# The last batch's operand loaded by ScalarE, and fewer conv taps ahead of the copies in stage 2

## The chip, the cores and the metric

The kernel runs on one core of one Trainium2 chip. The metric is the device time in microseconds (us) of one execution. TensorE (PE) multiplies matrices, VectorE (DVE) and ScalarE (ACT) work elementwise and empty the matmul results out of PSUM, GpSimd (POOL) does part of the elementwise work. DMAs are issued by the queue of an engine; in this kernel SyncE (SP) issues nearly all of them.

## The reference

Three layers follow one another on 4 batches. Cut to what matters here:

```python
def reference(...):                        # 4 batches
    a = attn(pooled q, k, v)               # 8 heads, 1152 keys, 576 pooled queries
    x = a as (4, 576, 512)
    # second layer: 4 experts, causal attention over 576 rows, two experts kept per row
    for e in range(4):
        q, k, v = x @ wq[e], x @ wk[e], x @ wv[e]
        ye = softmax(causal(scale * q @ k.T)) @ v @ wo[e]
        out += gate_weight(x, e) * ye
    # third layer: causal convolution of 5 taps as a gate
    gate = sigmoid(sum over k in 0..4 of conv_w[k] * out shifted down by 4 - k rows)
    return (gate * (out @ w_val)) @ w_out
```

## The kernel before

The program has three stages, one for each layer: pooled attention to about 476 us, the expert attention to about 693 us, and the gated product to the end. The change lies in stage 2.

**Stage 2** runs a loop over steps n = 0 to 39 and two more. A step is one batch b (ten steps), one pair of experts g (five steps) and one row tile i; the tiles come in the order 1, 3, 2, 4, 0. In a step the kernel first finishes the softmax weights of step n − 1 on DVE (`norm2`, L844 to L854; POOL then multiplies, L850), has PE make the scores of step n (L814, L821; DVE masks them at L823 and takes the row minimum at L824, L826), and has PE transpose the weights of step n − 2, whose results leave PSUM through `evac`: in turn by ACT (L862) and by DVE (L864, written COPY in the rows). Then come the exponentials of step n on ACT (L835, L837).

**Filler work.** Between these, PE works on a list `fill` of larger pieces, taken one by one by `pop()`: the projections of q and k (`proj`, L242, with the split of the result into a high part on ACT at L224 and a low part on DVE at L225), the values and gate logits (`vgate`, L276), the product with the values (`av2`, L901 and L914), and the product with wo that mixes the experts (`mix`, L936, emptied by ACT at L937 and L938). All of these use four PSUM buffers named a (`ps_m`), as do the transposes. What one piece leaves for other engines goes to the list `late2`, which the next `pop()` empties right behind its own PE work.

**Riders.** After a piece, `ride()` puts one small item on DVE: first what is in `urgent` (the gates, thirteen instructions L294 to L307), otherwise one item of `rides`, at most three in a step (`room = [3]`). The items of `rides` are the taps of the convolution (`tap`, L215), four for each of the four column groups m of a batch, put there when `mix` has finished a group (names x and gp), and a store of gp to memory (L947) in batches 0 and 1. `RD`, by n % 5, says whether the first piece of a step carries a rider at all; this piece stands between the scores and the transposes of the step. Before the change RD is (1, 0, 1, 1, 1).

**Loads and moves.** The operand of a batch, xh, is loaded from memory by `load2`, four DMAs of 576 KB (L196), one for each t. The results of `proj` are copied by `move` to the tiles of the scores: four DMAs for k (L256), six for q (L258, L260, L261 twice), all issued by SP in order. `proj(xh, g, then)` makes k first (w = 1), then q (w = 0). Where it was given `then`, it appends it to `late2` behind the move of q. It is given one only at n = 20, the second pair of batch 1 being over: `then` is `load2(3)`, the load of the last batch.

Of the kernel before, what the change touches and what calls it, by code (L numbers as in the profile page):

```python
# [20 lines left out]
def tile_kernel(ctx, tc, q, k, v, w_gate, wq, wk, wv, wo, w_val, conv_w, w_out, wo_t, q0, k0, out):  # L21
    nc = tc.nc
# [12 lines left out]
    pe, act, dve, pool = nc.tensor, nc.scalar, nc.vector, nc.gpsimd  # L35
# [8 lines left out]
                       fill=1.0, base=0, channel_multiplier=1)  # L44

    x_d = [dram.tile([P, KT, 2, SQ], F32R, name=f"x_d{b}") for b in range(B)]
# [6 lines left out]
                       fill=1e9, base=0, channel_multiplier=1)  # L53
# [10 lines left out]
    def f(ap):  # L64
        return ap.bitcast(F32)
# [124 lines left out]
            late.append(lambda n=n, t=t, c=c, whl=whl: nc.sync.dma_start(f(w3_d[n][:, t, :, c:c + HW]), f(whl)))  # L190
            yield

    def load2(b):
        xh = xh_p.tile([P, KT, 2, SQ], F32R, name="xh")
        for t in range(KT):
            nc.sync.dma_start(f(xh[:, t]), f(x_d[b][:, t]))  # L196
        return [[xh[:, t, i] for i in range(2)] for t in range(KT)]

    def load_part(b, tile_, k):
# [21 lines left out]
    late2, urgent, rides = [], [], []  # L221

    def split2(hi, lo, src, mul=1.0):
        act.activation(hi, src, AF.Copy, scale=mul)  # L224
        late2.append(lambda: dve.scalar_tensor_tensor(out=lo, in0=src, scalar=mul, in1=f(hi), op0=ALU.mult, op1=ALU.subtract))  # L225
# [3 lines left out]
    def proj(xh, g, then=None):  # L229

        box = {}

        def half(w, hf):
            if hf == 0:
                box[w] = hl2.tile([P, 2, SQ], F32R, name="hl")
            hl = box[w]
            cs = slice(w * ED + g * P, w * ED + (g + 1) * P)
            qsl = slice(hf * HQ, (hf + 1) * HQ)
            ps = ps_m.tile([P, 512], F32, name="a")
            ops = [(wi, xi, t) for t in range(KT) for wi, xi in THREE]  # L240
            for o, (wi, xi, t) in enumerate(ops):
                pe.matmul(ps[:, 0:HQ], lhsT=wqk[wi][:, t, cs], rhs=xh[t][xi][:, qsl], start=o == 0, stop=o == len(ops) - 1)  # L242
            split2(hl[:, 0, qsl], hl[:, 1, qsl], ps[:, 0:HQ], -scale if w == 0 else 1.0)
            if hf == 1:
                late2.append(lambda: move(w))
                if w == 0 and then:
                    late2.append(then)

        def move(w):
            hl = box[w]  # L250
            for r in range(2):
                rs = slice(64 * r, 64 * r + 64)
                for i in range(2):
                    src = hl[64 * i:64 * i + 64]
                    if w == 1:
                        nc.sync.dma_start(f(ks[g][i][rs]), f(src))  # L256
                    elif i == 0:
                        nc.sync.dma_start(f(qs[g][0][rs, 0:SQ]), f(src[:, r]))  # L258
                    else:
                        nc.sync.dma_start(f(qs[g][1][rs, 0:4 * P]), f(src[:, r, 0:4 * P]))  # L260
                        nc.sync.dma_start(f(qs[g][1][rs, SQ:]), f(src[:, r, 4 * P:]))  # L261

        return [(1.48, lambda w=w, hf=hf: half(w, hf)) for w in (1, 0) for hf in range(2)]

    def vgate(xh):
# [48 lines left out]
    fill = []  # L314
# [482 lines left out]
    with ExitStack() as s2l:  # L797
# [61 lines left out]
        def evac(dst, src):  # L859
            turn[0] += 1  # L860
            if turn[0] % 2:
                act.activation(dst, src, AF.Copy)  # L862
            else:
                dve.tensor_copy(dst, src)  # L864
# [86 lines left out]

        VG, FD, IN, FL, PEND, PN = 5, 1, 1, 2.6, 7, 3
        GM, VF = (0, 1, 2, 3), (0, 0, 0, 3, 1, 2, 2, 2, 2, 2, 2)
        RD = (1, 0, 1, 1, 1)
        ORDER = (1, 3, 2, 4, 0)
        steps = [(b, g, i) for b in range(B) for g in range(EP) for i in ORDER]
        LAG = 2
# [2 lines left out]
        def ahead(n):  # L960
            return (WORK[steps[n][2]][0] if n < len(steps) else 0) + (WORK[steps[n - LAG][2]][1] if LAG <= n < len(steps) + LAG else 0)
# [34 lines left out]
        for n in range(len(steps) + LAG):  # L996
            if n < len(steps):
                b, g, i = s = steps[n]
                if n % 5 == 0:
                    pts[b, g] = (pt_p2.tile([P, 4, 2, SQ], F32, name="pt"), pt_p2.tile([R64, 2, R64], F32, name="pt4"))  # L1000
                    if g == 0 and b:
                        fill += proj(xh[b], 1, (lambda: xh.update({3: load2(3)})) if b == 2 else None)
                        if b == B - 1:
                            fill.append((0, lambda: late2.append(begin3)))
                    if n == 10 * B - 5:
                        buf = [f(c2.tile([P, 2, SQ], F32R, name=f"k20{i}")) for i in range(2)]
                        bufs = [c2.tile([P, SQ + R64], F32R, name=f"q20{i}") for i in range(2)]
                        v2 = v_p.tile([P, 5, ED + E], F32, name="v2").rearrange("p t c -> p (t c)")
                        first3["raw"] = [[buf[t // 2][:, t % 2] for t in range(KT)], [f(bufs[t])[:, 0:SQ] if t < 2 else v2[:, (t - 2) * SQ:(t - 1) * SQ] for t in range(KT)]]
                        raws = [(0.74, lambda i=i, m=m, hf=hf: value(yhs, i, m, hf, lambda ps, m, qsl: evac(first3["raw"][i][m][:, qsl], ps))) for i in range(2) for m in range(KT) for hf in range(2)]  # L1010
                        fill += raws[0:14]
                    if b == 0 and g == 1:
                        buf = y0_p.tile([P, EP, 2, SQ], F32R, name="y0")
                        yhs.update({(0, i): buf[:, i] for i in range(EP)})
                    if b == 1 and g == 0:
                        buf = y12_p.tile([P, 2, EP, 2, SQ], F32R, name="y12")
                        yhs.update({(1 + j, i): buf[:, j, i] for j in range(2) for i in range(EP)})
                if n % 10 == 5 and b + 1 < B:
                    fill += proj(xh[b + 1], 0)
                if n % 10 == VG and b + 1 < B:  # L1020
                    v2s[b + 1], gws[b + 1], vg = vgate(xh[b + 1])
                    fill += vg
                if n == 0:
                    fill += proj(xh[0], 1)
                if n == FD:
                    fill += [(2.6, lambda g=g: fold(g)) for g in range(EP)]
            t = 0.0
            left = 5 - n % 5
            own = [ahead(m) for m in range(n, n + left)]
            budget = max(FL, (sum(c for c, _ in fill) + (PEND if 10 <= n and n % 10 < PN else 0) + sum(own)) / left) - own[0]  # L1030

            room = [3]

            def ride():
                if urgent:
                    urgent.pop(0)()
                    return
                if rides and room[0]:
                    room[0] -= 1
                    rides.pop(0)()  # L1040

            def pop(rider=True):
                c, a = fill.pop(0)
                now, late2[:] = late2[:], []
                a()
                for x in now:
                    x()
                if rider:
                    ride()
                return c  # L1050

            if 0 <= n - 1 < len(steps):
                norm2(steps[n - 1], gws[steps[n - 1][0]])
            for _ in range({0: 1, 5: 3}.get(n, 0)):
                t += pop()
            if n < len(steps):
                scores2(s)
            if fill:
                t += pop(RD[n % 5])
            else:  # L1060
                flush()
            if n >= LAG:
                b1, g1, i1 = steps[n - LAG]
                transp2(steps[n - LAG], pts[b1, g1])
                if i1 == ORDER[-1]:
                    if g1 == 1:
                        then = (lambda b1=b1: fill.extend(mix(b1, [yhs[b1, 0], yhs[b1, 1]]))) if b1 < B - 1 else begin_last
                    else:
                        then = (lambda: None) if b1 < B - 1 else load_wo3
                    fill[IN:IN] = av2(v2s[b1], pts[b1, g1], g1, yhs[b1, g1], then)  # L1070
            if n < len(steps):
                expo2(s)
            if n == 0:
                flush()
            while fill and t < budget:
                t += pop()
            ride()
            if n == 9:
                xh[2] = load2(2)
            if n in (12, 22):  # L1080
                flush()
            if n % 10 == 9:
                flush()
                while urgent:
                    urgent.pop(0)()
# [123 lines left out]
```

## Time and profile before

| | |
|---|---|
| median of three runs | 761.71 us (761.33 to 763.0) |
| the profiled execution | 761.71 us |
| its span in the trace | 759.9 us |
| granted TensorE clock | 1.0 |
| PE busy, share of the span | 98% |
| DVE busy | 75% |
| ACT busy | 59% |
| POOL busy | 42% |
| chain that ended last | 84% PE, 8% DVE, 3% DMA, 3% ACT |

A row of a timeline gives the start and the length in us, the engine, the line of the kernel, the operation, the tile written, an arrow, the tiles read, the shapes and a count; in brackets stands how long the engine idled just before and what it waited for. Rows of one engine can overlap a little.

### The profile page before, as it was taken

Reading aid. Unit: us, or ns where it says so; the run is one execution under the profiler, and the core shown is the slowest. Engines: PE = TensorE matmul, PEld = TensorE weight load, DVE = VectorE, ACT = ScalarE, POOL = GpSimd, SP = SyncE. Lnnn points to the kernel's source line nnn. Section 1 sums busy time; section 2 is a strip of 40 time slices with the busy share of each in tenths; the row PEclk is TensorE's granted clock in tenths of the full one; section 3 lists DMA queues with packets and bytes.
Section 4 is the critical chain, followed back from the end, with each engine's and each line's share of the span. In section 5 each row is a group of like instructions: output and inputs, shape, how many; then the busy total and the mean of one; then the engine's idle time right before and its main releaser. Section 6 shows DMA issues by size and latency. Waiting matters only on the chain.

```text
span 759.9 us, 14763 instructions
## 1 busy us (share of the span) xinstructions
PE 745.7 (98%) x5317; PEld 616.6 (81%) x5317; DVE 569.4 (75%) x1064; ACT 448.2 (59%) x985; POOL 316.3 (42%) x442
## 2 busy tenths in 40 slices
PE   8999999999999999999999999999999999999998
PEld 7787887787787787877878877988898888878887
DVE  6777888898888988756756766355889797988730
ACT  6665665665665756657656756334564654648632
POOL 6555675675676675652553501022322222220000
PEclk9999999999999999999999999999999999999999
DMA  7876878769778689666657581478425763800212
GB/s 258 254 174 203 226 190 255 211 195 261 209 227 250 187 262 258 178 204 208 166 164 227 132 286 48 111 210 189 135 54 141 199 159 81 267 1 15 84 57 97
DMA packets 83785, 133.52 MB, mean 176 GB/s; under 512 B 19072, under 2 KB 55424, under 8 KB 83712
## 3 DMA queue, kind: packets, MB, share of 16 engines
q1 hardware_dynamic: 83712, 132.58, 61.3%
q8 instruction: 42, 0.69, 0.4%
q14 instruction: 31, 0.25, 0.1%
HBM read 53.37 MB, written 21.76 MB: 99 GB/s over the span
## 4 chain that ended last, share of the span: by engine, by line
PE 84%; DVE 8%; DMA 3%; ACT 3%; issue 1%; SPq 0%; POOL 0%; POOLq 0%; ACTq 0%; DVEq 0%
PE s L440 21%; PE t L489 19%; PE t L519 18%; PE o L1120 7%; PE a L242 5%; PE a L275 4%; PE a L914 2%; DVE gp L215 2%; PE a L779 2%; PE s L814 2%; PE a L886 1%; DMA k<-hl 1%; PE t L478 1%; DVE nm L824 1%; DVE nm L445 1%
## 5 line engine op out<-in xcount | busy, mean ns | idle before, releaser
L452 ACT ACTIVATE p<-s,nm 128x1152 f32<-128x1152 f32 x144 | 176.2, 1223 | 87.9 <-DVE nm L445 85.8
L445 DVE TENSOR_REDUCE nm<-s 128x1 f32<-128x1152 f32 x144 | 192.1, 1352 | 13.9 <-PE s L440 13.6
L489 PE MATMUL t<-ident,p 128*128 128x128 f32 x1296 | 198.8, 275 | 0.7 <-DVE xf L521 0.4
L489 PEld LDWEIGHTS t<-ident,p 128*128 128x128 f32 x1296 | 149.1, 141 | 26.4 <-ACT pt L497 7.0
L497 ACT ACTIVATE pt<-t 128x384 f32<-128x384 f32 x223 | 102.1, 489 | 79.9 <-PE t L489 75.0
L519 PE MATMUL t<-pt,vn 128*64 128x256 f32 (+1 forms) x1152 | 146.7, 408 | 0.0
L499 DVE COPY pt<-t 128x384 f32<-128x384 f32 x209 | 110.9, 554 | 44.5 <-PE t L489 40.5
L519 PEld LDWEIGHTS t<-pt,vn 128*64 128x64 f32 x1152 | 80.0, 137 | 55.9 <-issue 5.2
L440 PE MATMUL s<-ka,qst 128*128 128x384 f32 x384 | 114.6, 380 | 0.2
L440 PE MATMUL s<-kb,qst 128*128 128x384 f32 x384 | 99.1, 367 | 1.7 <-ACT p L452 1.7
L850 POOL TENSOR_TENSOR p<-p,sm 128x512 f32<-128x512 f32 (+3 forms) x32 | 40.2, 1255 | 106.0 <-DVE sm L848 71.3
L440 PEld LDWEIGHTS s<-kb,qst 128*128 128x128 f32 x384 | 60.8, 189 | 15.7 <-issue 13.1
L440 PEld LDWEIGHTS s<-ka,qst 128*128 128x128 f32 x384 | 62.9, 190 | 1.1 <-DVE ka L574 0.9
L377 POOL TENSOR_TENSOR hlk<-kt,hlk 128x384 fp32r<-128x384 f32 x45 | 45.5, 1011 | 1.1
L521 DVE TENSOR_TENSOR xf<-t,rb 128x320 f32<-128x320 f32 (+1 forms) x32 | 14.6, 456 | 41.1 <-PE t L519 40.1
L467 POOL COPY rm<-rs 128x256 f32<-128x256 f32 x31 | 12.4, 401 | 79.3 <-DVE rs L462 77.7
L242 PE MATMUL a<-xh,wqk 128*128 128x288 f32 x288 | 43.3, 300 | 2.1 <-DVE pt L864 2.1
L835 ACT ACTIVATE p<-s,nm 128x256 f32<-128x256 f32 (+3 forms) x64 | 33.1, 524 | 20.3 <-DVE nm L824 20.3
L528 POOL CAST xt<-xf 128x320 fp32r<-128x320 f32 (+1 forms) x32 | 13.6, 426 | 69.9 <-DVE xf L521 69.3
L215 DVE SCALAR_TENSOR_TENSOR gp<-x,cw,gp 128x572 f32<-128x572 f32 (+3 forms) x48 | 40.4, 843 | 2.6 <-ACT gp L938 2.1
L242 PEld LDWEIGHTS a<-xh,wqk 128*128 128x128 f32 x288 | 39.4, 188 | 3.5 <-DVE pt L864 2.5
L440 PE MATMUL s<-hlk,mixed 128*128 128x384 f32 x135 | 33.7, 357 | 0.0
(193 smaller groups left out, 1170.8 us busy)
## 6 DMA issues: line engine op xcount, KB each, us to landing
ka<-hlk SPq DMA_DIRECT2D x90, 192.0 KB, 3.2
kb<-hlk SPq DMA_DIRECT2D x90, 192.0 KB, 3.7
vn<-in_v_dram SPq DMA_DIRECT2D x16, 576.0 KB, 7.2
k<-hl SPq DMA_DIRECT2D x32, 288.0 KB, 4.9
kt<-in_k_dram SPq DMA_DIRECT2D x15, 576.0 KB, 6.1
qt<-in_q_dram SPq DMA_DIRECT2D x15, 576.0 KB, 5.2
qst<-hlq SPq DMA_DIRECT2D x60, 128.0 KB, 3.2
xh<-x_d SPq DMA_DIRECT2D x12, 576.0 KB, 6.0
```

Source lines behind the costliest of these rows:

```text
L215: dve.scalar_tensor_tensor(out=gp[:, n:], in0=x[:, 0:SQ - n], scalar=cw[:, m, c:c + 1], in1=gp[:, n:], op0=ALU.mult, op1=ALU.add)
L242: pe.matmul(ps[:, 0:HQ], lhsT=wqk[wi][:, t, cs], rhs=xh[t][xi][:, qsl], start=o == 0, stop=o == len(ops) - 1)
L377: late.append(lambda: pool.tensor_tensor(out=hlk[:, 1, gs], in0=kt[:, gs], in1=f(hlk[:, 0, gs]), op=ALU.subtract))
L440: pe.matmul(ps[:, 0:GW], lhsT=ops[c][0], rhs=ops[c][1], start=c == 0, stop=c == len(ops) - 1)
L445: dve.tensor_reduce(d["nm"], d["s"][:, :, 0:GW], axis=AX.XY, op=ALU.min)
L452: act.activation(d["p"], d["s"][:, :, 0:GW], AF.Exp, bias=d["nm"], scale=-1.0, accum_out=sums[(2 * n + u) % len(sums)][:, i:i + 1])
L489: pe.transpose(ps[:, j * P:(j + 1) * P], p[:, g, j * P:(j + 1) * P], ident)
L497: act.activation(dst, src, AF.Copy)
L499: dve.tensor_copy(dst, src)
L519: pe.matmul(ps[64 * h:64 * h + 64, 0:N], lhsT=vn[:, h, j, :], rhs=pt[:, j, h, :], start=j == 0, stop=j == C - 1)
L850: pool.tensor_tensor(out=pv, in0=pv, in1=sm[:, :, None].to_broadcast([P, 2, w]), op=ALU.mult)
L1120: pe.matmul(ps[:, 0:w], lhsT=hl[xi][:, kt, t * P - a:(t + 1) * P - a], rhs=end3["wo3"][:, kt, wi, c:c + w], start=o == 0, stop=o == len(op ...
```

## The change

Four edits, all in stage 2:

- `load2` takes the queue to issue from, and the load of the last batch is given ACT's.
- In `proj`, `then` is called at once, when the piece with the second half of q is issued, and no longer put behind the move of q.
- The last entry of `RD` is 0: the first piece of a step with n % 5 = 4 carries no rider.
- `room` is 2 and no longer 3 in the steps with n % 10 of 3 and 4, so that at most two riders go there.

```diff
-    def load2(b):
+    def load2(b, queue=nc.sync):
...
-            nc.sync.dma_start(f(xh[:, t]), f(x_d[b][:, t]))
+            queue.dma_start(f(xh[:, t]), f(x_d[b][:, t]))
...
                 late2.append(lambda: move(w))
                 if w == 0 and then:
-                    late2.append(then)
+                    then()
...
-        RD = (1, 0, 1, 1, 1)
+        RD = (1, 0, 1, 1, 0)
...
-                        fill += proj(xh[b], 1, (lambda: xh.update({3: load2(3)})) if b == 2 else None)
+                        fill += proj(xh[b], 1, (lambda: xh.update({3: load2(3, act)})) if b == 2 else None)
...
-            room = [3]
+            room = [2 if n % 10 in (3, 4) else 3]
```

How the instructions stand on the engines, before and after. The first place is DVE around the end of n = 14, in batch 1 (the numbers behind x are those of the tile). Before:

```order
L215 SCALAR_TENSOR_TENSOR gp<-x_7180,cw,gp 128x572
L215 SCALAR_TENSOR_TENSOR gp<-x_7180,cw,gp 128x573
L215 SCALAR_TENSOR_TENSOR gp<-x_7180,cw,gp 128x574
L844 TENSOR_SCALAR sm<-sm 128x1
L845 RECIPROCAL sm<-sm 128x1
...
L823 TENSOR_TENSOR s<-s,cmask 128x2x128
L824 TENSOR_REDUCE nm<-s 128x2
L215 SCALAR_TENSOR_TENSOR gp<-x_7180,cw,gp 128x575
L864 COPY pt<-a 128x3x128
```

The same place on DVE after the change:

```order
L215 SCALAR_TENSOR_TENSOR gp<-x_7180,cw,gp 128x572
L215 SCALAR_TENSOR_TENSOR gp<-x_7180,cw,gp 128x573
L844 TENSOR_SCALAR sm<-sm 128x1
L845 RECIPROCAL sm<-sm 128x1
...
L823 TENSOR_TENSOR s<-s,cmask 128x2x128
L824 TENSOR_REDUCE nm<-s 128x2
L864 COPY pt<-a 128x3x128
L215 SCALAR_TENSOR_TENSOR gp<-x_7180,cw,gp 128x574
L215 SCALAR_TENSOR_TENSOR gp<-x_7180,cw,gp 128x575
```

Two taps have gone from ahead of the copy of the transposes to behind it. The second place is DVE around the gates (L294 to L307), half a batch later, where the last column group's taps stand (x_7284 before, x_7283 after). The difference, in two pieces:

```order
-L215 SCALAR_TENSOR_TENSOR gp<-x_7284,cw,gp 128x574
 L864 COPY pt<-a 128x3x128
-L215 SCALAR_TENSOR_TENSOR gp<-x_7284,cw,gp 128x575
-L294 TENSOR_TENSOR gt<-v_7308 128x80
...
+L215 SCALAR_TENSOR_TENSOR gp<-x_7283,cw,gp 128x572
+L215 SCALAR_TENSOR_TENSOR gp<-x_7283,cw,gp 128x573
+L294 TENSOR_TENSOR gt<-v_7306 128x80
...
 L824 TENSOR_REDUCE nm<-s 128x2
+L215 SCALAR_TENSOR_TENSOR gp<-x_7283,cw,gp 128x574
 L864 COPY pt<-a 128x8x64
 L225 SCALAR_TENSOR_TENSOR hl<-a,hl 128x288
+L215 SCALAR_TENSOR_TENSOR gp<-x_7283,cw,gp 128x575
```

The last two taps of the batch, which stood ahead of the gates, now stand behind them. The third place is the start of batch 2 (n = 20 and on), on SP, the queue that issues the moves of k and q, and on ACT. SP, the difference:

```order
-L947 DMA g_d_71<-gp 128x576 x2
-L256 DMA k_6178<-hl 64x1152
...
-L258 DMA q_6174<-hl 64x576
-L260 DMA q_6175<-hl 64x512
...
-L196 DMA xh<-x_d_70 128x1152 x4
...
+L256 DMA k_6179<-hl 64x1152
+L947 DMA g_d_71<-gp 128x576
+L258 DMA q_6174<-hl 64x576
```

The four loads are gone from behind the q moves, and one store of gp stands between the k and the q moves. ACT there:

```order
 L835 ACTIVATE p,sm<-s,nm 128x512 x2
 L224 ACTIVATE hl<-a 128x288
+L196 DMA xh<-x_d_70 128x1152 x4
 L902 ACTIVATE y_7003<-a 128x128
 L224 ACTIVATE y_7003<-a 128x448
```

The four loads have come in ahead of the first product with the values (L902). In the changed program the first, third and fifth q moves wait for the completion counter of the first, second and third of these loads, the second, fourth and sixth for that of a k move.

## Rows read from the trace of the kernel before

**Rows 1.** Windows: us; busy time (instructions) by engine; granted clock, DMA share, GB/s.

```profile
564.00:611.00 47.00, 45.81 (x350) 41.29 (x350) 40.92 (x104) 25.94 (x79) 12.34 (x10) 1.00 0.57 152
```

**Rows 2.** Timeline of PE in stage 2: start, length, line, [wait before].

```profile
561.32 1.86 PE L242 MATMUL a<-xh,wqk 128*128 128x288 f32 x12 [1.05 <-DVE pt L864]
...
593.34 0.44 PE L901 MATMUL a<-pt,v 128*64 128x128 f32 x4
...
608.32 2.06 PE L242 MATMUL a<-xh,wqk 128*128 128x288 f32 x12 [1.06 <-DVE pt L864]
...
640.58 0.44 PE L901 MATMUL a<-pt,v 128*64 128x128 f32 x4
...
658.84 1.06 PE L779 MATMUL a<-y,wf 128*128 128x288 f32 x6 [1.07 <-DVE pt L864]
...
681.33 0.44 PE L901 MATMUL a<-pt,v 128*64 128x128 f32 x4 [0.61 <-DVE pt L864]
```

**Rows 3.** Timeline of PE's weight loads around 606 to 610.

```profile
606.49 0.56 PEld L814 LDWEIGHTS s<-k,q 128*128 128x128 f32 x4
...
609.71 0.43 PEld L242 LDWEIGHTS a<-xh,wqk 128*128 128x128 f32 x3 [0.17 <-DMA xh<-x_d]
```

**Rows 4.** Timeline of DVE from 555 to 593, in batch 1.

```profile
555.73 2.52 DVE L215 SCALAR_TENSOR_TENSOR gp<-x,cw,gp 128x572 f32<-128x572 f32 x3 [1.05 <-ACT gp L938]
558.16 0.15 DVE L844 TENSOR_SCALAR sm<-sm 128x1 f32<-128x1 f32 x1
...
559.70 1.09 DVE L215 SCALAR_TENSOR_TENSOR gp<-x,cw,gp 128x575 f32<-128x575 f32 x1
560.72 0.55 DVE L864 COPY pt<-a 128x384 f32<-128x384 f32 x1
...
584.61 0.24 DVE L294 TENSOR_TENSOR gt<-v 128x80 f32<-128x80 f32 x1 [0.29 <-ACT v L276]
...
589.94 0.17 DVE L844 TENSOR_SCALAR sm<-sm 128x2 f32<-128x2 f32 x1 [0.26 <-ACT p L835]
...
592.39 0.41 DVE L864 COPY pt<-a 128x256 f32<-128x256 f32 x1
```

**Rows 5.** Timeline of DVE at the end of stage 2.

```profile
646.09 0.17 DVE L844 TENSOR_SCALAR sm<-sm 128x2 f32<-128x2 f32 x1 [1.20 <-ACT p L835]
...
665.10 0.29 DVE L920 TENSOR_TENSOR hl<-a,hl 128x128 fp32r<-128x128 f32 x1 [1.01 <-ACT hl L902]
...
676.17 0.14 DVE L844 TENSOR_SCALAR sm<-sm 128x1 f32<-128x1 f32 x1
```

**Rows 6.** Timeline of ACT at the start of batch 2.

```profile
593.83 0.28 ACT L902 ACTIVATE y<-a 128x128 fp32r<-128x128 f32 x1
596.46 0.55 ACT L224 ACTIVATE y<-a 128x448 fp32r<-128x448 f32 x1 [2.34 <-PE a L914]
...
601.17 0.74 ACT L837 ACTIVATE p<-s,nm 128x576 f32<-128x576 f32 x1 [0.81 <-DVE nm L826]
```

**Rows 7.** Timeline of SP's queue there: DMA issues.

```profile
592.50 3.19 SPq L256 DMA_DIRECT2D k<-hl  x4
...
600.32 2.92 SPq L196 DMA_DIRECT2D xh<-x_d  x4
```

**Rows 8.** Line L196: ns of an issue (min/median/max), first and last start; landing.

```profile
L196 SPq DMA_DIRECT2D xh<-x_d x12: 430/528/1442, 437.7 to 602.8; - x12
...
DMA to landing us min/median/max: 4.5/6.0/8.2
```

**Rows 9.** Line L260, part of the q moves: time to landing.

```profile
DMA to landing us min/median/max: 2.4/4.5/8.7
```

**Rows 10.** Windows as in group 1, at the start of batch 2.

```profile
596.00:598.00 2.00, 2.00 (x19) 1.86 (x18) 0.84 (x2) 1.51 (x4) 0.38 (x1) 1.00 1.06 244
...
602.00:604.00 2.00, 2.00 (x17) 1.76 (x16) 1.23 (x2) 2.00 (x8) 0.00 (x0) 1.00 0.82 172
...
606.00:608.00 2.00, 1.26 (x10) 1.05 (x9) 1.97 (x4) 1.12 (x6) 1.15 (x1) 1.00 1.02 419
```

## The prediction

> **What bounds the kernel now.** Read first the busy times of one stretch of stage 2, about as long as a batch [rows 1]: of 47 us TensorE (PE) is busy 45.81, at a granted clock of 1.00, and VectorE (DVE) 40.92. So PE is the bound and only its few waits can be won. The timeline of PE then shows where these are [rows 2]: 1.05 us at 561.32, 1.06 us at 608.32 and 1.07 us at 658.84, each for a copy of transposes (L864) on DVE. I call them waits A, B and C. All three fall in the five steps that mix the batch before; that is where the taps run. Their sum, 3.18 us, is 0.42% of the time. A fourth item hangs on B: the first weight load of the xh operand waits 0.17 us for its DMA [rows 3], and the group of 12 matmuls at 608.32 takes 2.06 us where the same at 561.32 takes 1.86, so 0.20 us for the late load.
>
> Read next what DVE does ahead of such a copy [rows 4]. At 555.73 it starts three taps, later runs a fourth at 559.70, and only then the copy at 560.72. From there DVE waits for almost nothing: 0.29 us at 584.61 ahead of the gates and 0.26 at 589.94, up to the copy at 592.39 that the PE row L901 at 593.34 needs. DVE is thus nearly full over these 37 us, and what is postponed ahead of the copy is owed to PE further on.
>
> **Part by part: the taps (the order in batches 1 and 2).** No tap is added or dropped, so the work is equal. By the order, the third of the three taps and the fourth leave the place ahead of the copy. One tap takes 0.81 us start to start (555.73 to 558.16, three of them) and the fourth 1.02 (559.70 to 560.72), in all 1.83. The copy can start at 560.72 − 1.83 = 558.89, and PE, ready for L242 at 561.32 − 1.05 = 560.27, finds it done (558.89 + 0.55 + 0.05 of hand-over = 559.49). Wait A goes whole, −1.05, with 0.78 to spare.
>
> What is late next: two taps now stand behind the gates instead of ahead of them. The gates start at 584.61 when ACT brings the last projection; this comes 1.05 earlier, at 583.56, while DVE, with two taps less (1.62), would be there at 584.32 − 1.62 = 582.70. So DVE idles 0.86 there instead of 0.29: it cannot use the time that was won. Behind the gates it has 1.62 more to do and loses the idle 0.26 at 589.94. The copy of 592.39 then starts at 592.39 − 1.05 + 1.62 − 0.26 = 592.70, and L901 at 592.70 + 0.41 + 0.05 = 593.16. Before, it started at 593.34, 0.49 after the earliest time that the copy allowed. So of the 1.05 some 0.87 is given back and **batch 1 is worth −0.18**. The ends: −1.05 if the debt is covered by something I do not see, and about 0 if the taps cost a little more.
>
> Batch 2 has the same pattern, down to L901 at 640.58 [rows 2]: −1.06 − 0.20 + 0.87 = **−0.39**, if the load costs nothing.
>
> **Batch 3.** From 646 on DVE is busy without a gap but for 1.01 us at 665.10, where it waits for what ACT makes of L901's output [rows 5]. Two taps move from ahead of wait C and of that gap to behind it, ahead of the norm at 676.17 on which the last transposes and L901 at 681.33 depend [rows 2]. DVE's total up to that norm is equal. PE comes earlier by 1.07 and so shortens nothing at the end: DVE reaches the norm at the same time, as long as its gap stays near 1.01. I take **0**; the ends are −1.07 (gain kept, the gap filled) and +0.6 (two taps, 1.65, less 1.07, if what DVE waits for at 665.10 comes earlier by wait C alone).
>
> **The load on ACT.** Four issues leave SP, where they stood behind the q moves at 600.32 [rows 7], and stand on ACT between the L224 before 593.83 and L902. ACT then has a gap of 2.34 us before 596.46, where it waits for PE [rows 6]: this is the cover. What an issue costs on ACT no row of before shows; the nearest rows are the twelve of the same shape on SP, 0.430/0.528/1.442 us [rows 8], and the four at 600.32 took 0.73 each. At 0.528 the four end at 593.83 + 2.11 = 595.94 and L902 follows by 596.2: covered. At 0.73 they end at 596.75, L902 at 597.03, the next row is 0.57 late, and the 0.81 that ACT idles before 601.17 [rows 6] takes up most, with 0.2 to 0.4 reaching PE meanwhile. At 1.442 the row is 3.4 late and 2.6 remain. Behind the issues on ACT are L902, the L224 for y and the exponentials; who waits for them are DVE (L920, and by it the q moves) and PE. I take **x = +0.1**, ends 0 and 2.6.
>
> **The moves.** The eight completion counters of the DMAs go round: in the changed program the first, third and fifth of the six q moves wait until the first, second and third load have landed, and the second, fourth and sixth for k moves. Before, no move waited for a load. SP runs in order, so behind a held q move stand all that follow. PE needs the moves for the scores at 606.49 [rows 3]. A load landed 4.5/6.0/8.2 us after its issue [rows 8], a q move 2.4/4.5/8.7 [rows 9]. The third load, issued by 594.9, is there at 600.9 by the median, and the fifth q move 4.5 later, 605.4: nothing is lost. By the longest load and the median q it is 594.9 + 8.2 + 4.5 = 607.6, 1.1 late. By bytes: the moves ran at 244 GB/s, the loads alone at 419, with a dip to 172 between them at 602 to 604 [rows 10], and PE stopped waiting for the load at 609.71 [rows 3]. If mixing makes nothing faster, the last q move ends about there, 609.71 − 606.49 = 3.2 late, less the part of the dip that is filled, (419 − 172) / 419 of 2 us or 1.2 at most, half of it taken: 2.6, say 2.5. If it makes the stretch faster, the moves are in time. I take **s = +0.5**, nearer to the medians, with ends 0 and 2.5 here (5.3 in rival 2).
>
> The Trainium skill, "DMA: Bandwidth & Descriptors", section "Issuing engines are not separate DMA queues", speaks against a free early load: DMAs of all issuing engines run on the same 16 engines and interleave, and issuing from a second one saves only the sequencer's time. By it s would lie toward 2.5 and the sum toward 763.7; the trace of before, where moves and loads hardly overlap, neither shows nor excludes it.
>
> One store of gp now stands between the k and the q moves, and waits for the first k move. The buffer it frees is wanted by a later L938; I cost it at nothing, covered by the whole row of mixes in between.
>
> **Sum:** −0.18 − 0.39 + 0 + 0.1 + 0.5 = +0.03. The profiled execution took 761.71 us (span 759.9), which is also the median of the three runs, so the forecast is 761.7.
>
> **The rivals.**
> 1. *The gains stay.* The debt of two taps finds cover: then −1.05 − 1.26 − 1.07 = −3.4, 758.3, and with one of the three given back 759.4. For it: the waits before are plain and the copy gets 0.78 to spare. Against it: DVE had only 0.55 us of idle time in 37, and ahead of the gates it cannot run ahead. It decides if L901 near 593 waits for nothing. 18%.
> 2. *The q moves come late.* The slower side, in one place: the first scores of batch 2's second pair, at 606.49. With s = 2.5 the sum is −0.18 − 0.39 + 0.1 + 2.5 = +2.0, 763.7; with the longest load and the longest q move, 594.9 + 8.2 + 8.7 = 611.8, s is 5.3 and the time 766.5. It decides from s of about 2. For it: the counters tie the moves to the loads, and one stretch carries the same bytes. Against it: the medians. The skill's rule above is this rival's. 16%.
> 3. *The issues on ACT are long.* At 1.442 each, x = 2.6 and s = 0.5 give 764.2; for it speaks only the longest of twelve rows. 6%.
> 4. *The load stays late for what B needs,* or B's copy is held by something else: then −0.18 + 0.1 + 0.5 = +0.4 and up to 762.1, which is no change either. 10%, inside "same".
>
> **How the numbers follow.** A measurement of this kernel can tell about 0.2%, 1.5 us, from no change: faster is below 760.2, slower above 763.2. The forecast with rival 4 has 60%, of which a few hundredths spill to either side: same 0.56. Faster gets rival 1's 0.18 and 0.04 of spill: 0.22. Slower gets rivals 2 and 3: 0.22. For 8 in 10 the range reaches from a mixed case of rival 1 (two of the three gains half kept, about −2) to rival 2 with x = 0.4: −0.57 + 2.5 + 0.4 = +2.3. So 759.6 to 764.1.
>
> **What the changed profile would show.** Right: no PE wait of 1 us near 561, 608 and 658; the copy ahead of the last taps; idle time of DVE ahead of the gates near 0.9; and a new wait of PE at L901 near 593 and 640 of 0.8 to 0.9 for a copy on DVE; the norm near 676 within half a microsecond of its old time. For the load: four issues on ACT inside the gap before the L224 for y, and the xh landed well ahead of 608. Wrong would be: PE waiting more than 1 us at L814 near 606 for a DMA of q (rival 2), L902 and the next rows of ACT over 1 us late (rival 3), or no new wait at L901 at all (rival 1). Least certain is s, a meeting of loads and moves that no stretch of before shows.

## The result: slower by 0.7%

The changed kernel takes 767.24 us (median of 6 runs, 766.62 to 769.09) against 761.67 us before; the ratio is 1.0072 with a 95% interval of 1.0059 to 1.0084. The forecast was 761.7, "no change", with a range that ended at 764.1. The profiled execution took 766.68 us, its span is 765.0 and its mean granted clock 0.996.

The timeline of PE after the change, the rows that answer to [rows 2] and the first of [rows 3] (start, length, line, in brackets the wait ahead):

```profile
559.22 0.63 PE L814 MATMUL s<-k,q 128*128 128x256 f32 x4
...
564.33 1.76 PE L242 MATMUL a<-xh,wqk 128*128 128x288 f32 x12
...
568.51 0.44 PE L901 MATMUL a<-pt,v 128*64 128x128 f32 x4
...
592.23 0.44 PE L901 MATMUL a<-pt,v 128*64 128x128 f32 x4 [0.55 <-DVE pt L864]
...
603.43 2.65 PE L936 MATMUL a<-y,wos 128*128 128x288 f32 x18
610.18 1.19 PE L814 MATMUL s<-k,q 128*128 128x256 f32 x4 [4.10 <-DMA q<-hl]
611.17 3.08 PE L242 MATMUL a<-xh,wqk 128*128 128x288 f32 x12
614.05 1.27 PE L874 MATMUL a<-ident,p 128*128 128x128 f32 x5
...
617.89 1.76 PE L242 MATMUL a<-xh,wqk 128*128 128x288 f32 x12
...
622.09 0.44 PE L901 MATMUL a<-pt,v 128*64 128x128 f32 x4
...
645.81 0.44 PE L901 MATMUL a<-pt,v 128*64 128x128 f32 x4 [0.54 <-DVE pt L864]
...
666.94 0.44 PE L901 MATMUL a<-pt,v 128*64 128x128 f32 x4 [0.84 <-DVE pt L864]
...
683.17 1.07 PE L779 MATMUL a<-y,wf 128*128 128x288 f32 x6 [1.70 <-DVE q L864]
...
686.30 0.44 PE L901 MATMUL a<-pt,v 128*64 128x128 f32 x4 [0.61 <-DVE pt L864]
```

Waits A, B and C are gone. In their place stands one wait of 4.10 us at 610.18, at the first scores of batch 2's second pair, for a q move. Behind it the same work is slower: four matmuls of L814 take 1.19 us where they take 0.63 at 559.22, the twelve of L242 3.08 where [rows 2] has 1.86 and 2.06. The windows show why (columns as in [rows 1]; the third number from the end is the granted clock):

```profile
606.00:608.00 2.00, 0.08 (x1) 0.00 (x0) 1.64 (x5) 1.13 (x5) 0.09 (x1) 1.00 1.06 282
608.00:610.00 2.00, 0.00 (x0) 0.00 (x0) 0.00 (x0) 1.19 (x3) 0.53 (x1) 0.71 0.68 163
610.00:612.00 2.00, 1.82 (x8) 1.85 (x9) 0.56 (x2) 0.00 (x0) 0.00 (x0) 0.50 0.28 108
612.00:614.00 2.00, 2.00 (x10) 2.00 (x9) 0.57 (x1) 0.00 (x0) 0.00 (x0) 0.50 0.00 0
614.00:616.00 2.00, 2.00 (x12) 1.95 (x11) 0.86 (x2) 1.06 (x5) 0.00 (x0) 0.58 0.00 0
616.00:618.00 2.00, 2.00 (x14) 1.82 (x13) 1.93 (x5) 0.94 (x4) 0.00 (x0) 1.00 0.00 0
```

PE is idle from 606 to 610, the granted clock falls to 0.50, that is from 2.4 to 1.2 GHz, and is back at 1.00 by 616, after PE has worked for some 5 us.

Where the time went, by the starts of seven of the eight groups of L901 (one for each pair and batch), before and after:

| L901 | before | after | shift | change of the shift |
|---|---|---|---|---|
| batch 0, first pair | 526.17 | 525.76 | −0.41 | (before the change acts) |
| batch 1, first pair | 570.24 | 568.51 | −1.73 | −1.32, wait A gone |
| batch 1, second pair | 593.34 | 592.23 | −1.11 | +0.62, the debt of two taps |
| batch 2, first pair | 617.47 | 622.09 | +4.62 | +5.73, the q move and the half clock, less wait B |
| batch 2, second pair | 640.58 | 645.81 | +5.23 | +0.61, the debt again |
| batch 3, first pair | 663.42 | 666.94 | +3.52 | −1.71, wait C gone, and more |
| batch 3, second pair | 681.33 | 686.30 | +4.97 | +1.45, the wait at 683.17 |

(The rows are the matmuls of L901 at the starts named in [rows 2] and above; 526.17, 570.24 and 617.47 before and 525.76 after are other rows of the same line.) Batch 1 gains 0.70, and batch 3 gives back all but 0.26. The first steps gain more than the length of the waits. For A, the start of L814 and that of L242 behind it lie 0.47 us apart after (559.22 and 559.69), 1.69 before (559.63 and 561.32), and the twelve of L242 take 0.10 less: 1.32 in all. Around C 1.34 comes in this way, and the rest of the 1.71 from short pauses of PE just ahead of it, at L779 and L874, that are gone too.

The loss is batch 2's, above all the 5.73 us. The stretch from L901 at 593.34 to the next took 24.13 us before, of which 1.26 were wait B and the late load; after it takes 29.86, of which 4.10 are the wait. The rest grew by 29.86 − 4.10 − (24.13 − 1.26) = 2.89 us. Most of this is the price of the half clock: from L814 at 610.18 to the third L242 behind it at 617.89 are 7.71 us, and the same groups of batch 1, at full clock, take 5.11 (559.22 to 564.33), so 2.60. The other 0.3 lies in the main ahead of the wait, where the issues on ACT delay PE a little; this comes back under x below.

What SP and ACT issued there, the rows that answer to [rows 7] and [rows 6]:

```profile
591.88 3.78 SPq L256 DMA_DIRECT2D k<-hl  x4
596.04 0.33 SPq L947 DMA_DIRECT2D g_d<-gp  x1
597.97 0.46 SPq L258 DMA_DIRECT2D q<-hl  x1
599.76 0.46 SPq L260 DMA_DIRECT2D q<-hl  x1
603.02 0.46 SPq L261 DMA_DIRECT2D q<-hl  x1
603.58 0.54 SPq L258 DMA_DIRECT2D q<-hl  x1
605.89 0.46 SPq L260 DMA_DIRECT2D q<-hl  x1
606.40 0.60 SPq L261 DMA_DIRECT2D q<-hl  x1
```

```profile
591.58 0.69 ACT L835 ACTIVATE p<-s,nm 128x512 f32<-128x512 f32 x1 [1.96 <-DVE nm L824]
591.99 0.37 ACTq L196 DMA_DIRECT2D xh<-x_d  x1
...
592.26 0.68 ACT L835 ACTIVATE p<-s,nm 128x512 f32<-128x512 f32 x1
592.39 0.69 ACTq L196 DMA_DIRECT2D xh<-x_d  x1
...
593.12 2.56 ACTq L196 DMA_DIRECT2D xh<-x_d  x2
595.72 0.28 ACT L902 ACTIVATE y<-a 128x128 fp32r<-128x128 f32 x1 [2.40 <-PE a L914]
595.90 0.54 ACT L224 ACTIVATE y<-a 128x448 fp32r<-128x448 f32 x1
```

Behind this, a weight load of PE waits for ACT (PEld, as in [rows 3]):

```profile
602.73 0.31 PEld L886 LDWEIGHTS a<-ident,p 128*128 128x128 f32 x3 [0.32 <-ACT gp L938]
```

The loads leave between 591.99 and 595.7, together with the k moves. The q moves leave between 597.97 and 606.40, the last of them 6.8 us later than before. Issue to landing, from the table of DMA issues of 590 to 614 (KB each, median us to landing):

```profile
xh<-x_d ACTq DMA_DIRECT2D x4, 576.0 KB, 11.7
k<-hl SPq DMA_DIRECT2D x4, 288.0 KB, 8.5
...
q<-hl SPq DMA_DIRECT2D x2, 144.0 KB, 8.8
```

The same loads took 5.5, the k moves 4.6 and these q moves 4.7 in that stretch before. All of them took about twice as long.

### The profile page after: what moved, and what is told of

Read it like the earlier page. It is cut to its first block, busy times and chain, and to the rows that moved or that the text cites. A ratio compares the mean times of both kernels' runs of the same rounds, so it can differ in the third digit from the quotient of the medians.

```text
span 765.0 us, 14752 instructions
## 1 busy us (share of the span) xinstructions
PE 747.5 (98%) x5317; PEld 618.7 (81%) x5317; DVE 567.7 (74%) x1064; ACT 448.1 (59%) x985; POOL 316.1 (41%) x442
## 4 chain that ended last, share of the span: by engine, by line
PE 86%; DVE 7%; ACT 3%; DMA 1%; issue 1%; ACTq 0%; SPq 0%; POOLq 0%; DVEq 0%
PE s L440 21%; PE t L489 19%; PE t L519 18%; PE o L1120 7%; PE a L242 5%; PE a L275 4%; PE a L914 2%; PE a L779 2%; PE s L814 2%; PE a L886 2%; DVE gp L215 1%; PE t L478 1%; PE a L936 1%; DMA q<-hl 1%; ACT p L835 1%
## 5 line engine op out<-in xcount | busy, mean ns | idle before, releaser
L445 DVE TENSOR_REDUCE nm<-s 128x1 f32<-128x1152 f32 x144 | 192.1, 1352 | 13.9 <-PE s L440 13.5
L242 PE MATMUL a<-xh,wqk 128*128 128x288 f32 x288 | 44.6, 306 | 0.0
L242 PEld LDWEIGHTS a<-xh,wqk 128*128 128x128 f32 x288 | 41.1, 196 | 0.8 <-issue 0.4
```

The costliest lines, as they stand in the source:

```text
L445: dve.tensor_reduce(d["nm"], d["s"][:, :, 0:GW], axis=AX.XY, op=ALU.min)
```

## The experiments

Times are medians in us; the ratio is to the kernel before, run beside it.

| kernel | time | ratio (95%) | PE waits near 606 to 611 | last landing that PE waited for |
|---|---|---|---|---|
| before | 761.6 to 762.0 | | 1.06 copy, 0.17 load | 609.7 |
| changed | 767.24 | 1.0072 (1.0059 to 1.0084) | 4.10 q move | 610.2 |
| taps alone | 764.14 | 1.0034 (1.0020 to 1.0048) | 2.02 load | 609.8 |
| taps alone, again | 764.94 | 1.0032 (1.0011 to 1.0053) | 1.70 load | 611.0 |
| load alone | 766.26 | 1.0058 (1.0045 to 1.0071) | 2.72, cause not named, q by its place | 610.8 |
| at once, on SP | 766.30 | 1.0054 (1.0037 to 1.0070) | 4.56 q move | 610.4 |
| on ACT, behind q | 766.65 | 1.0055 (1.0040 to 1.0071) | 1.31 q move (and 2.08 for ACT at 601 and 603) | 611.6 |
| at once, on POOL | 767.11 | 1.0062 (1.0043 to 1.0081) | 4.71 q move, by the weight load's row | 610.5 |
| two loads at once | 764.75 | 1.0038 (1.0020 to 1.0056) | 1.77 q move, 1.01 load | 610.5 |
| RD alone | 761.09 | 0.9989 (0.9979 to 0.9999) | 1.21 load | 609.4 |
| RD alone, first load amid q | 761.25 | 0.9991 (0.9982 to 1.0001) | 1.10 load | 609.3 |
| RD alone, store in the burst | 761.79 | 0.9993 (0.9979 to 1.0008) | 1.34 load | 610.1 |

**Taps or load?** The first kernel is the one before with the two rider edits only:

```diff
-        RD = (1, 0, 1, 1, 1)
+        RD = (1, 0, 1, 1, 0)
...
-            room = [3]
+            room = [2 if n % 10 in (3, 4) else 3]
```

> The two rider edits alone (RD and room); the load stays on SP behind the q moves. Theory 1 (the early load makes the q moves late; the taps are harmless): no wait of PE at L814 near 606 over 0.5 us; waits A and C go as in the changed kernel, L901 near 593 comes 0.7 earlier; B's wait for the copy goes too, but PE then meets the load, which lands at 609.7 as before, so that most of B and A is lost there: 760.5 to 761.5. Theory 2 (the postponed taps cost): over 764.

The second is the one before with the load alone:

```diff
-                    late2.append(then)
+                    then()
...
-                        fill += proj(xh[b], 1, (lambda: xh.update({3: load2(3)})) if b == 2 else None)
+                        fill += proj(xh[b], 1, (lambda: xh.update({3: load2(3, act)})) if b == 2 else None)
```

> The load alone: on ACT and at once, RD and room as before. Theory 1: PE waits for a q move at L814 near 606 for 3 to 4.5 us and then runs at half clock for some us; wait B goes, A and C stay: 765.5 to 768. Theory 2 (taps): 761 to 762.5.

The load alone is enough for most of the loss, 766.26, as the first theory expected, and its clock fell to 0.50 from 612 to 614; its wait of 2.72 was a little under the 3 to 4.5, as PE reaches the place later with wait A kept. The taps alone were expected at 760.5 to 761.5 by the first theory and came to 764.14: a miss, just on the mark of the second. So the tap edits alone cost some 2.5 us, the load alone 4.6 and both 5.6; they do not add up, since both end in the same place. Is it the postponed work that costs, as the second theory has it? The profiled execution of the taps alone, 762.2 and so one of its shorter ones, shows where the gain of A and B goes. Its PE timeline:

```profile
602.99 2.65 PE L936 MATMUL a<-y,wos 128*128 128x288 f32 x18
...
606.99 0.66 PE L242 MATMUL a<-xh,wqk 128*128 128x288 f32 x3 [0.49 <-DMA xh<-x_d]
608.42 0.66 PE L242 MATMUL a<-xh,wqk 128*128 128x288 f32 x3 [0.77 <-DMA xh<-x_d]
609.84 0.67 PE L242 MATMUL a<-xh,wqk 128*128 128x288 f32 x3 [0.76 <-DMA xh<-x_d]
```

PE reaches the projection of the last batch 2.4 us earlier than before (its first three matmuls start at 605.95, not at 608.32) and there waits 0.49 + 0.77 + 0.76 = 2.02 us for the loads, one after the other. The debt at L901 is 0.55 there, as in the changed kernel. That was expected, and it would leave the time about where it was. For the rest a second profile was taken.

> The two rider edits alone once more, for a second profile: their executions lay between 761.5 and 767.3 with a granted clock of 0.993 to 1.0. If the spread is the clock after PE's waits for xh: a profile above 763 shows half clock for some us from about 608 on and the other stretches as in the first profile. If it is something else: the loss stands in another stretch.

That execution took 764.94. Its PE timeline and windows:

```profile
609.59 0.66 PE L242 MATMUL a<-xh,wqk 128*128 128x288 f32 x3 [0.77 <-DMA xh<-x_d]
611.00 1.02 PE L242 MATMUL a<-xh,wqk 128*128 128x288 f32 x3 [0.75 <-DMA xh<-x_d]
...
612.74 2.63 PE L242 MATMUL a<-xh,wqk 128*128 128x288 f32 x12
```

```profile
608.00:610.00 2.00, 1.07 (x6) 0.84 (x6) 1.74 (x6) 1.25 (x4) 0.61 (x1) 1.00 1.02 419
610.00:612.00 2.00, 1.25 (x6) 1.01 (x6) 0.00 (x0) 0.00 (x0) 0.00 (x0) 0.78 0.43 168
612.00:614.00 2.00, 2.00 (x11) 1.97 (x10) 1.09 (x3) 1.28 (x5) 0.00 (x0) 0.50 0.00 0
614.00:616.00 2.00, 2.00 (x13) 1.87 (x12) 1.90 (x5) 0.72 (x3) 0.00 (x0) 0.87 0.00 0
```

With one of 0.18 at 608.16 the waits come to 1.70 us, 2.02 in the first profile, but now the clock falls to 0.50, and twelve matmuls of L242 take 2.63. So the clock fell after 1.70 us of waits cut in three as well as after one wait of 4.10, in some executions and not in others: over the 19 runs of this kernel the times go from 761.46 at a clock of 1.000 to 767.57 at 0.993. From L901 of batch 1 to L901 of batch 2 this execution takes 26.65 us (593.67 to 620.32), the first profile 25.40 (592.19 to 617.59). That is 1.25 of the 2.7 us between the two spans; the other 1.47 is there at L901 of batch 0 already (527.19 and 525.72), ahead of all that this section treats. What the clock did in the longest runs of this kernel, which left no profile, is only seen in their mean; the last experiment comes back to it.

**Counters, queue or bytes?** The forecast named a shared counter as the cause of a late q move. Three kernels change the queue and the counters and leave the changed tap order. On SP at once:

```diff
-                        fill += proj(xh[b], 1, (lambda: xh.update({3: load2(3, act)})) if b == 2 else None)
+                        fill += proj(xh[b], 1, (lambda: xh.update({3: load2(3)})) if b == 2 else None)
```

> The changed kernel with the load at once but on SP, so that it stands in one queue between the k and the q moves, and only the last two q moves wait for a load's counter. If it is the bytes ahead of the q moves that count: q late by 3 to 6 us, 765.5 to 769. If it is the queue (ACT, and what stands behind the issues on it) or the waits for counters: 761 to 763.5.

On ACT, behind the q moves:

```diff
-                    then()
+                    late2.append(then)
```

> The changed kernel with the load on ACT but put behind the q moves, as before; it is issued some 3 us later, behind L902 and the L224 for y. By the built order the third and the fifth q move still wait for the counter of the first and second load. If the counters hold the q moves: q late by 2 to 4 us, 763.5 to 766.5. If it is the order in which the bytes are asked for, with nothing held by the counters: q in time, 760 to 761.5.

At once, on POOL:

```diff
-                        fill += proj(xh[b], 1, (lambda: xh.update({3: load2(3, act)})) if b == 2 else None)
+                        fill += proj(xh[b], 1, (lambda: xh.update({3: load2(3, nc.gpsimd)})) if b == 2 else None)
```

> The changed kernel with the load issued by POOL instead of ACT, at once as there; by the built order no q move then waits for the counter of a load. Theory 1a (bytes: the burst of moves and loads ends near 610 in any order, and what stands last in it is late): q late by 2.5 to 5 us at L814 near 606, 765 to 768. Theory 1b (the counters hold the q moves): q issues follow each other as before, wait at L814 under 1 us, 760 to 762.5.

The rows of PE in the first and the third of these, with the weight load's row of the third:

```profile
610.41 1.19 PE L814 MATMUL s<-k,q 128*128 128x256 f32 x4 [4.56 <-DMA q<-hl]
```

```profile
610.49 1.22 PE L814 MATMUL s<-k,q 128*128 128x256 f32 x4 [4.71 <-DMA g_d<-gp]
610.49 0.93 PEld L814 LDWEIGHTS s<-k,q 128*128 128x128 f32 x4 [4.94 <-DMA q<-hl]
```

On SP only the last two q moves wait for a load's counter; on POOL none does. The wait is 4.56 and 4.71 all the same. So neither ACT's queue nor a load's counter is needed for it; the bytes ahead of the q moves are enough. On POOL the first three q moves were issued one behind the other at 595.64 to 596.78, and landed 13.2 to 13.5 us later. By the rule of the Trainium skill weighed in the prediction ("DMA: Bandwidth & Descriptors", section "Issuing engines are not separate DMA queues") the queue should not matter, and the trace agrees: 4.10, 4.56 and 4.71 us from ACT, SP and POOL. The issues still stretch with POOL, since the last q moves wait for the counters of k moves, which landed 11.0 us after issue there: late bytes hold the next issue in any case.

On ACT behind q the wait for q is only 1.31, but the four issues held ACT for 3.89 us, PE waited 1.32 and 0.76 us (2.08) for ACT's work, and the result is as slow: a miss for the favourable side, and 0.15 above the other's range. The order that its edit asks for did not come about in time: on ACT's own queue the loads left from 596.59 to 600.48, the q moves on SP only from 597.33 on. And the counters act here. The third q move left at 603.55, just as the first load landed (7.0 us after its issue), and the fifth at 607.43. So this kernel does not tell the bytes from the counters, and what the counters add on top of the bytes was not measured apart.

The last column of the table carries the reading. Whatever the order, the burst of moves, store and loads begins with the k moves near 592 and ends at 609.3 to 611.6, 17 to 19 us later. What stands last in it is what PE waits for. Before, that was the load, and PE needed it last and piece by piece.

**How many bytes?** The changed kernel with two loads at once and two behind the q moves:

```diff
+        early = KT if queue is nc.sync else 2
-        for t in range(KT):
+        for t in range(early):
             queue.dma_start(f(xh[:, t]), f(x_d[b][:, t]))
+        if early < KT:
+            late2.append(lambda: [nc.sync.dma_start(f(xh[:, t]), f(x_d[b][:, t])) for t in range(early, KT)])
```

> The changed kernel, but only the first two loads go at once on ACT; the other two stand behind the q moves on SP. By the built order the third and fifth q move still wait for a load's counter. By bytes: two loads less ahead of the q moves is 1.18 MB, 2.8 us at 419 GB/s, so the wait at L814 falls from 4.1 to about 1.3 (0.5 to 2): 763 to 765. If the counters hold the q moves whatever the bytes: over 3 us, 766 to 768.

```profile
607.04 0.92 PE L817 MATMUL s<-k,q 128*128 128x256 f32 x4 [1.77 <-DMA q<-hl]
...
610.45 0.66 PE L245 MATMUL a<-xh,wqk 128*128 128x288 f32 x3 [1.01 <-DMA xh<-x_d]
```

The wait for q is 1.77, inside 0.5 to 2, and the time 764.75 inside 763 to 765, though the profiled execution is the fastest of its ten, 762.82. The other two loads are then late by 1.01. In this kernel too the third and fifth q moves wait for a load's counter (the fifth was held until 602.90), and the wait shrank as the bytes ahead did: the amount ahead sets it.

**Is there a better order?** RD alone, the tap between the row minimum and the copy goes behind the copy, and nothing else moves:

```diff
-        RD = (1, 0, 1, 1, 1)
+        RD = (1, 0, 1, 1, 0)
```

> RD alone: only the one tap between the row minimum and the copy goes behind the copy; the three taps ahead and all that follows stay as before, the load too, and the store of gp stays out of the burst. Expected by the debt theory: waits A and B fall to about 0, nothing is owed at L901 near 593, so -1.0 from A; the burst shifts with PE and B's 1.06 is mostly lost again to the load: 760.3 to 761.0. If the taps matter in another way: 761.5 or more.

The same with the first load between the halves of the q moves (`then[0]` loads t = 0, and `then[1]`, put behind the moves, the other three):

```diff
...
             for r in range(2):
+                if w == 0 and then and r == 1:
+                    then[0]()
...
```

> As the kernel with RD alone, and the first of the four loads stands on SP between the first three and the last three q moves, so that the dip of the DMA rate at 602 to 604 is filled. Theory 1a (bytes and their order): the burst ends about 1 us earlier, the q moves are still in time, PE's waits for xh near 607 go down by some 1 us: 759.3 to 760.3. If any load ahead of a q move makes it late: a wait at L814 near 606 of over 1 us, 761.5 to 764.

RD alone measured 761.09, 0.09 above what was expected, a ratio of 0.9989 whose interval just excludes 1: the best of all, though by 0.1% only. Its PE timeline:

```profile
607.99 0.66 PE L242 MATMUL a<-xh,wqk 128*128 128x288 f32 x3 [0.47 <-DMA xh<-x_d]
609.39 0.66 PE L242 MATMUL a<-xh,wqk 128*128 128x288 f32 x3 [0.74 <-DMA xh<-x_d]
...
658.23 1.06 PE L779 MATMUL a<-y,wf 128*128 128x288 f32 x6 [0.79 <-DVE pt L864]
```

Wait A is gone without a new wait at L901; B became 0.47 + 0.74 at the load; C is still there with 0.79. The first load amid q did not improve on it (761.25, above its range): with one load early the other three still end at 609.3, and PE is paced by these. It shows that one load ahead of half of the q moves does no harm.

The last kernel puts the store of gp where the two rider edits put it, into the burst:

```diff
...
+            while w == 1 and held:
+                held.pop()()
...
-                steps.append(lambda: late2.append(lambda: nc.sync.dma_start(g_d[b][:, m], gp)))
+                store = lambda: nc.sync.dma_start(g_d[b][:, m], gp)
+                steps.append(lambda: held.append(store) if (b, m) == (0, KT - 1) else late2.append(store))
```

> The kernel with RD alone, and only the last store of gp of batch 0 moved: it is held back until the k moves of batch 2 are issued, where the two rider edits put it by themselves. No tap is postponed. If the store (288 KB, some 1.2 us at 240 GB/s) is what makes the taps-only kernel slow: PE's waits for xh near 607 to 610 grow from 1.2 to 2 us or more and the clock falls in some executions: 762 to 764. If it is the postponed taps: 760.5 to 761.5, as with RD alone.

It measured 761.79: between the two theories, below the first one's range and above the second's. PE's waits are 1.34, and in 3 of its 11 runs the mean clock is 0.997 or 0.998; in the 12 of RD alone it is 0.999 at the least, but the kernel before has 3 runs of 26 at 0.998, so the count says little. The store costs at most some tenths, not clear of nothing by the two intervals.

It does not make up the 3 us between RD alone and the two rider edits together. In the two profiles whose clock did not fall (spans of 759.3 and 760.5) 1.2 us of them is there, most of it by L901 of batch 2 (640.24 and 641.32): PE waits longer for the loads and for DVE's copies. The rest goes with the clock: 15 of the 19 runs of the two rider edits have a mean of 0.998 or less, none of the 12 of RD alone. One place where it falls is the loads, shown above. There is a second. At the end of batch 3 PE waits some 1.7 us for a copy on DVE at L779, in every profile of a kernel with both rider edits and in none with RD alone or the load alone. In the profile of the load at once on SP, 767.23 with a mean clock of 0.993, the clock falls behind this wait as well:

```profile
684.00:686.00 2.00, 2.00 (x10) 1.49 (x8) 0.92 (x4) 0.68 (x2) 0.61 (x1) 0.50 0.00 0
```

On ACT behind q it falls only there. It costs some 0.6 us: from L901 of batch 3 to the first L936 behind its second pair are 27.48 and 27.54 us in these two, 26.90 in the changed kernel. How the two places share the spread of the two rider edits is not shown.

## Why the prediction was wrong

- **What bounds the kernel, and waits A, B and C:** right. All three went. Their worth was taken a little too small, 1.05 for A where 1.32 came.
- **The debt of the taps:** right in kind. At L901 near 592 and 645 PE waits 0.55 and 0.54 for a copy, where 0.8 to 0.9 was forecast; of the gain 0.62 is given back and not 0.87, and batch 1 is worth −0.70, not −0.18. The DVE idle of 0.9 ahead of the gates did not come: the copy ahead of the gates waited 0.56 for PE instead, and the gates started at once.
- **Batch 3:** right, −0.26 for a forecast of 0. The place was another: DVE hands its debt to PE at L779 (1.70 us at 683.17), for the copy of a projection in the queue behind the taps.
- **The issues on ACT, x = +0.1:** inside its ends, but 0.4. They took 0.37 to 1.73 us each, the last two long, and L902 started only at 595.72; DVE's L920 waited 1.00 us for it, and by this chain PE's weight load at 602.73 waited 0.32 for ACT. The taps alone, which differ only in the load, have the same L901 at 592.19 instead of 592.23 and the L936 of 603.43 at 602.99, so 0.40. It cost nothing in the end, since PE stood waiting for q behind it. (With the load alone 0.22 us goes back to L902.)
- **The moves, s = +0.5: this is the step that failed.** s was 4.1. I set it near the medians of landing times that were measured with nothing beside them, although the text held the other reckoning: the burst ends at 609.7 in any order, PE needs the q moves at 606.5, 3.2 late. That bound I then cut to 2.5 by a dip that was to be filled. The dip was filled, and an added store of 288 KB, which I had costed at nothing, took its place; PE came 0.4 earlier as well. 610.18 − 606.08 = 4.10. (The store is not needed for a wait: the load alone, without it in the burst, has 2.72.)
- **No term for the clock.** I priced a wait at its length. The 4.10 us cost 2.60 more at half clock. This alone is more than the 2.4 from the forecast to the end of the range.
- **The gain of B** was counted as −1.26 with the load landing in time once it was early. Left where it was, the load takes the gain back (2.02 us of waits in the taps alone), and put ahead, it takes it from the q moves. Both ends follow from one sum of bytes, which was never set against PE's new arrival.
- **Rival 2** is what happened: the place holds, and of its two grounds the bytes; the counters turned out not to be needed. That its worse end, 766.5, comes near the measured time is luck: its s of 5.3 was too long by 1.2, and it had no term for the clock either. It had 16% because the medians were weighed against it.

## What to carry to other kernels

Before a transfer is moved ahead, add up the bytes of the whole burst it stands in: if the DMA engines are full from its start to its end, moving one transfer up only chooses which consumer is late, and the one needed last should stay last. Landing times taken from quiet stretches are no price for a crowded one. A new wait of PE of some microseconds is to be priced with the time at half clock behind it (it came in every profile with one wait of 2.7 to 4.7 us), and an engine freed on the compute side should be checked against the next transfer that it will meet.

## What the runs showed of the hardware

- Waits that break up PE's work can halve its clock for some us: 0.50 from 610 to 614 after 4.1 us of waiting, and, in some executions only, after three waits of 0.2 to 0.8 us or one of 1.70. The sum of the waits does not tell: it fell after 0.18, 0.77 and 0.75 and not after 0.49, 0.77 and 0.76. The taps alone, with such waits, spread over 6 us from run to run, where of 26 runs of the kernel before 22 keep within 2.
- An ACT issue does not wait its turn behind the arithmetic ahead of it: the first load left at 591.99, while the exponential of 591.58 ran and before the exponential at 592.26, which stands ahead of it in the program. So an issue on ACT can start earlier than its neighbours' times suggest, here 1.8 us ahead of the 593.83 on which the prediction reckoned, of which 0.6 is that ACT's rows came earlier (the L224 before it at 592.92 and not 593.54).
- Moves, store and loads together were carried at 256 to 304 GB/s between 596 and 604 (windows of 2 us of the changed kernel), where the moves alone ran at 244 [rows 10] and loads alone at over 400. Mixing them did not shorten the burst: with the load alone, which has the same bytes as before and began 0.15 us later, PE's last wait for it ended at 610.8, before at 609.7.
